# Low attention scores of the odd head pairs in the other two quadrants of TensorE, and their part of y behind U

## The chip, the cores and the metric

The kernel runs on one core of one Trainium2 chip. The metric is device time in microseconds (us), the median of several executions; lower is better. PE is TensorE, DVE VectorE, ACT ScalarE, POOL GpSimd, SP SyncE.

## What is computed

A gated linear attention of 4 sequences with 8 heads of 48 channels over 768 steps, and two MLPs on its output, all in fp32:

```python
for t in range(S):                       # state: 48x48 per head
    state = alpha[t][:, None] * state + k[t] (outer) v[t]
    y[t] = q[t] @ state
x = y                                    # 3072 tokens x 384
x = (h - tanh(h)) @ w_out                # h = x @ w_in, 384 -> 2048 -> 384
out = leaky(x @ w2_in) @ w2_out          # slope alpha2 per channel for h < 0
```

## The kernel before

**Tiles.** Attention is done in 24 tiles: tile g holds 128 time steps of one of the four sequences, with its 8 heads as four pairs (p = 0 to 3); of a pair, head u = 0 has its channels in partitions 0 to 63 and head u = 1 in 64 to 127. The steps of a tile are done at once: running products of alpha (`attn_a1`, `attn_a2`) scale q on POOL (L235) and k on DVE (L247), so that plain matmuls do the rest:
- scores (`attn_sc`): k against q, then on DVE a causal mask (`attn_m`), which gives P;
- y (`attn_y`): the state of the tiles before times q, plus v times P;
- the update U of the state (`attn_u`): k times v, then on DVE the new state (`attn_s`);
- x: y is copied on ACT (`attn_xh`, L445) and what the copy rounded off is taken on DVE (`attn_xl`, L452).

Tiles 8 to 23 are the halved ones (`halved`). There the 128x128 scores of a head are three 64x64 blocks; the fourth would be masked away. The late 64 steps against both halves of the earlier ones are the high scores (L284). The early 64 steps against themselves are the low scores (L288).

**Places on PE.** PE's array is used in parts: a matmul with 64 rows of k and 64 columns of result takes one of four quadrants, told by the partitions that it reads (rows) and those of PSUM that it writes (columns). High scores go round all four. Low scores of head u read partitions 64u and write partitions 64u, so that they use two, the other two stay unused. For y, 64x32 tiles hold the first 32 channels of a head against the state (L383) and against the low scores (L391, with `vlow`, a copy of v's early steps laid out for both halves), and 128x32 tiles hold the rest (L396 to L405) and U (L437).

**PSUM.** Banks 0, 1, 2 are used whole by the halved tiles (`shared`); high scores lie in banks 1 and 2, low scores in bank 0, y in 1 and 2, U in 0. Banks 3 to 7 belong to the MLPs.

**Order.** Every engine works through its instructions in the order of the program, which is written out by hand: a loop over steps of the MLPs (`steps`), of each nine matmuls for h (`mm_h`, L552) and nine of the step two back into the accumulators (`mm_acc1`, L607), with the attention put between by two tables. `vec` is run ahead of the step's elementwise work and holds the scans of the next tile, `mid` behind it and holds scores, y and U. For tiles 8 to 11 `attn_a` of tile g + 1 stands in `vec` of the step whose `mid` has `piece_c` of tile g (y, U, x, state). For later tiles it stands three steps ahead of `piece_c`, and the scores of tile g + 1 stand right ahead of y of tile g.

```python
at(vec, s + 1 if j == 2 else s if g == 3 * B else s - 1, attn_a, g + 1)
at(mid, s + (1 if j == 2 else 2), piece_c, g)
```

Of the kernel before, what the change touches and what calls it, by code (L numbers as in the profile page):

```python
# [10 lines left out]
F32 = mybir.dt.float32  # L11
# [3 lines left out]
ALU = mybir.AluOpType  # L15
# [8 lines left out]
NP = H // 2  # L24
# [24 lines left out]
def c_place(h):  # L49

    return h if h < 4 else 4 + (h % 4 ^ 1)
# [84 lines left out]
def emit_all(nc, tc, const, qkav, vlow, vt, w1, w2, alpha2, cst, out):  # L136
    c = {}
    c["masks"] = const.tile([128, CH + CH // 2], F32, name="masks")
    c["mask"], c["mlow"] = c["masks"][:, 0:CH], c["masks"][:, CH:]
    c["ident"] = const.tile([128, 128], F32, name="ident")  # L140
    c["d1a"] = const.tile([128, AW], F32, name="d1a")
    c["d1s"] = const.tile([128, AW], F32, name="d1s")
    c["al2"] = const.tile([128, KF], F32, name="al2")
    c["nal"] = const.tile([128, KF], F32, name="nal")
    c["lim"] = const.tile([128, 3], F32, name="lim")
    c["out_of"] = const.tile([128, 2 * NTILE + 2 * KF + 1], F32, name="out_of")
    c["sums"] = const.tile([128, 2 * KF], F32, name="sums")
    c["guard"] = const.tile([128, 4], F32, name="guard")
    c["flag"] = const.tile([1, 1], U32, name="flag")

    with tc.tile_pool(name="x2d", bufs=1, space=DRAM) as dp:
        x2d = [dp.tile([128, KC, N2], F32, name=f"x2d{j}") for j in range(NB)]
        c["bad2d"] = dp.tile([128, 1], F32, name="bad2d")
        engines = mybir.EngineType
        tc.mark_branch_hint_location("general", "LikelyTaken",
                                     [engines.PE, engines.SP, engines.Activation, engines.DVE])
        emit_fast(nc, tc, qkav, vlow, w1, w2, alpha2, cst, out, x2d, c)

    with tc.If(c["bad"] > 0, label="general"):
        emit_general(nc, tc, qkav, vt, w1, w2, c["al2"], cst, out)  # L160


def emit_fast(nc, tc, qkav, vlow, w1, w2, alpha2, cst, out, x2d, c):
# [14 lines left out]
    def bank(i, shape, name):  # L178
        return ps.tile(shape, F32, tag=f"bank{i}", name=name)
# [82 lines left out]
    def shared(b):  # L262

        if b not in shared_t:
            shared_t[b] = bank(b, [128, 512], "all")
        return shared_t[b]

    def attn_banks(g):

        if g < B:  # L270
            return ((7, 2, 3, 3)[g], (5, 6) if g % 2 == 0 else (0, 1), (7, 2)[g // 2], 256 * (g % 2))
        if g < 2 * B:
            return 5, (6, 7), 5, 0
        return 0, (1, 2), 0, 0

    def attn_sc(g):
        _, q, k, _ = qk_t[g]
        if halved(g):
            scs = st[g, "sc"] = [shared(b)[:, 0:NP * HC].rearrange("s (p t) -> s p t", p=NP) for b in (1, 2, 0)]
            for p in range(NP):  # L280
                for u in range(2):
                    r = 64 * u
                    for t in (0, HC):
                        nc.tensor.matmul(scs[u][t:t + HC, p], k[r:r + 64, p, t:t + HC], q[r:r + 64, p, HC:CH],  # L284
                                         start=True, stop=True)
            for p in range(NP):
                for r in (0, 64):
                    nc.tensor.matmul(scs[2][r:r + 64, p], k[r:r + 64, p, 0:HC], q[r:r + 64, p, 0:HC],  # L288
                                     start=True, stop=True)
            return  # L290
        scs = [bank(b, [128, NP, CH], f"sc{u}") for u, b in enumerate(attn_banks(g)[1])]
        for p in range(NP):
            for u in range(2):
                r = 64 * u
                nc.tensor.matmul(scs[u][:, p], k[r:r + 64, p], q[r:r + 64, p], start=True, stop=True)
        st[g, "sc"] = scs
# [32 lines left out]
    def last_tile(g):  # L329
        return g >= NTILE - B  # L330

    HC = CH // 2
    vl_t = {}

    def halved(g):
# [4 lines left out]
    def load_vlow(g):  # L340
# [2 lines left out]
        vl = vl_t[g] = bp.tile([128, NP, 64], F32, tag="vlow", name="vlow")  # L343
        nc.sync.dma_start(vl.rearrange("s p e -> s (p e)"), vlow[g - 2 * B])

    def attn_m(g):
        scs = st.pop((g, "sc"))
        if halved(g):
            tiles = [bp.tile([128, 2, NP, HC], F32, tag="P0", name="P0"), bp.tile([128, 1, NP, HC], F32, tag="P1", name="P1")]
            st[g, "P", 0], st[g, "P", 1], st[g, "P", 2] = P = tiles[0][:, 0], tiles[1][:, 0], tiles[0][:, 1]  # L350
            for i, m in enumerate((mask[:, HC:CH], mask[:, HC:CH], mlow)):
                nc.vector.tensor_tensor(P[i], scs[i], m[:, None, :].to_broadcast([128, NP, HC]), op=ALU.mult)
            return
        for u in range(2):
            P = bp.tile([128, NP, CH], F32, tag=f"P{u}", name=f"P{u}")
            nc.vector.tensor_tensor(P, scs[u], mask[:, None, :].to_broadcast([128, 4, CH]), op=ALU.mult)  # L356
            st[g, "P", u] = P

    def attn_y(g):
        _, q, _, v = qk_t[g]  # L360
# [4 lines left out]
        if first:  # L365
            y = bank(b0, [128, KC, CH], "y")
            parts = st[g, "y"] = ((y, slice(0, KC)),)
            y = [y[:, ct] for ct in range(KC)]
        else:
            if halved(g):  # L370
                even, odd = (shared(b)[:, 256:256 + n * CH].rearrange("r (n t) -> r n t", n=n)
                             for b, n in ((1, 2), (2, 1)))
            else:
                even, odd = bank(b0, [128, 2, CH], "y"), bank(b1, [128, 1, CH], "y")
            st[g, "y"] = (even, slice(0, KC, 2)), (odd, slice(1, 2))
            y = [even[:, 0], odd[:, 0], even[:, 1]]

        if not first:
            for i in range(4):
                for ct in range(2):  # L380
                    h = c_place(4 * ct + i)
                    p, r = h // 2, 64 * (h % 2)
                    nc.tensor.matmul(y[ct][32 * i:32 * i + 32], Sp[r:r + 64, p, 0:32], q[r:r + 64, p],  # L383
                                     start=True, stop=False)
        if halved(g):
            vl, Pl = vl_t.pop(g), st.pop((g, "P", 2))
            for i in range(4):
                for ct in range(2):
                    h = c_place(4 * ct + i)
                    p, r = h // 2, 64 * (h % 2)  # L390
                    nc.tensor.matmul(y[ct][32 * i:32 * i + 32, 0:HC], vl[r:r + 64, p, 0:32], Pl[r:r + 64, p],  # L391
                                     start=False, stop=False)
            for ct in range(2):
                for i in range(4):
                    h = c_place(4 * ct + i)
                    nc.tensor.matmul(y[ct][32 * i:32 * i + 32, HC:CH], v[:, h // 2, h % 2, 0:32], P[h % 2][:, h // 2],  # L396
                                     start=False, stop=(ct == 1))
            for u in range(2):
                for p in range(NP):
                    nc.tensor.matmul(y[2][32 * p:32 * p + 32, HC:CH], v[:, p, u, 32:64], P[u][:, p],  # L400
                                     start=False, stop=False)
            for p in range(NP):
                nc.tensor.matmul(y[2][32 * p:32 * p + 32, 0:HC], vl[:, p, 32:64], Pl[:, p], start=False, stop=False)
            for p in range(NP):
                nc.tensor.matmul(y[2][32 * p:32 * p + 32], Sp[:, p, 32:64], q[:, p], start=False, stop=True)  # L405
            return
        for ct in range(2):
            for i in range(4):
# [13 lines left out]
    def attn_u(g):  # L422
        if last_tile(g):
            return
        v = qk_t[g][3]
        knat = st.pop((g, "knat"))
        _, _, b, o = attn_banks(g)
        if halved(g):
            u_bank[b] = shared(b)
            o = 256  # L430
        elif o == 0:
            u_bank[b] = bank(b, [128, 512], "U")
# [530 lines left out]

    def close(g):
        attn_y(g)
        attn_u(g)
        attn_xh(g)


# [318 lines left out]
def pack(inputs):  # L1288
# [20 lines left out]
    vlow = vp.reshape(NTILE, CH, NP, 2, 64)[2 * B:, 0:CH // 2].transpose(0, 3, 1, 2, 4).reshape(-1, CH, NP * 64)  # L1309
# [30 lines left out]
```

## Time and profile before

| | |
|---|---|
| median of 3 runs | 887.82 us (887.74 to 888.15) |
| the profiled execution | 888.66 us |
| its span in the profile | 886.8 us |
| PE busy | 876.6 us (99%) |
| DVE, ACT, POOL busy | 639.7 (72%), 485.3 (55%), 90.4 us (10%) |
| chain that ended last: PE, DVE, ACT | 89%, 6%, 2% |

A row of the timeline gives the start and the length of a run of like instructions on one engine; lengths of matmuls are modelled, so that matmuls are read by their starts. An fp32 matmul is two records. PEld is the load of weights into PE.

### The profile page before, as it was taken

What the parts mean: (1) busy time and instruction counts of PE and PEld (TensorE: products, weight loads), DVE (VectorE), ACT (ScalarE), POOL (GpSimd) and SP (SyncE); (2) the same over time, 40 slices, a digit from 0 to 9 for tenths busy, and PEclk for the clock granted to TensorE, in tenths of its full rate; (3) what the DMA queues carried; (4) which work ended last, traced back from release to release, by engine and by line L of the source; (5) the groups of instructions that cost most, each with busy time, mean ns of one, the idle gap of its engine ahead of it and who ended that gap; (6) DMA issues with size and microseconds to landing.
All of it is one profiled execution on the core that took longest, in us unless ns stands there. A gap on an engine that the chain in (4) does not pass through costs nothing.

```text
span 886.8 us, 16995 instructions
## 1 busy us (share of the span) xinstructions
PE 876.6 (99%) x6960; PEld 726.5 (82%) x6966; DVE 639.7 (72%) x1120; ACT 485.3 (55%) x908; POOL 90.4 (10%) x89
## 2 busy tenths in 40 slices
PE   8999999999999999999999999999999999999997
PEld 5678887888888888888888888888888888888886
DVE  8998996777556665553467798796867776867774
ACT  3565645555656566533677664454554554554542
POOL 2100000110000100000125234010010010010000
PEclk9999999999999999999999999999999999999999
DMA  9675003345455544300563211001001000100001
GB/s 335 257 294 223 1 1 87 104 123 174 138 169 189 179 142 140 121 7 10 202 211 119 103 77 36 36 1 37 36 2 36 36 8 30 36 1 1 36 1 37
DMA packets 34946, 83.70 MB, mean 94 GB/s; under 512 B 15409, under 2 KB 17970, under 8 KB 32306
## 3 DMA queue, kind: packets, MB, share of 16 engines
q1 hardware_dynamic: 21906, 79.28, 24.9%
q10 hardware_dynamic: 12960, 3.31, 2.0%
q8 instruction: 55, 0.90, 0.4%
q14 instruction: 25, 0.20, 0.1%
HBM read 70.00 MB, written 9.44 MB: 90 GB/s over the span
## 4 chain that ended last, share of the span: by engine, by line
PE 89%; DVE 6%; ACT 2%; DMA 1%; issue 1%; ACTq 0%
PE h L552 41%; PE acc L607 20%; PE o L749 18%; PE o L628 4%; PE all L284 1%; DVE iA L245 1%; DMA qv<-qkav 1%; DVE cv L102 1%; PE all L288 1%; DVE P L356 1%; DVE cv L101 1%; DVE A L233 1%; PE all L383 1%; PE all L396 1%; PE all L437 1%
## 5 line engine op out<-in xcount | busy, mean ns | idle before, releaser
L552 PE MATMUL h<-x,w 128*128 128x512 f32 x1728 | 489.9, 391 | 0.0
L552 PEld LDWEIGHTS h<-x,w 128*128 128x128 f32 x1728 | 324.1, 188 | 68.8
L607 PE MATMUL acc<-g,w 128*128 128x512 f32 x864 | 214.9, 393 | 0.3 <-ACT x2e L616 0.3
L607 PEld LDWEIGHTS acc<-g,w 128*128 128x128 f32 x864 | 160.2, 188 | 35.3 <-issue 0.8
L749 PE MATMUL o<-g,w 128*128 128x256 f32 (+1 forms) x625 | 172.6, 335 | 0.0
L590 DVE TENSOR_TENSOR g<-gb,g 128x512 fp32r<-128x512 f32 x120 | 85.7, 714 | 53.1 <-ACT g L585 52.6
L749 PEld LDWEIGHTS o<-g,w 128*128 128x128 f32 x625 | 111.9, 188 | 14.5
L585 ACT CAST g<-gb 128x512 fp32r<-128x512 f32 x120 | 74.5, 621 | 89.7 <-DVE gb L567 56.4
L567 DVE TENSOR_TENSOR gb<-h,ga 128x512 f32<-128x512 f32 x96 | 66.1, 689 | 73.9 <-ACT ga L566 73.3
L749 PE MATMUL o<-g,ws 128*128 128x256 f32 x408 | 113.8, 279 | 0.0
L573 DVE SCALAR_TENSOR_TENSOR gb<-h,ga 128x512 f32<-128x512 f32 x80 | 55.2, 690 | 70.1 <-ACT ga L572 70.1
L572 ACT ACTIVATE ga<-h,nal 128x512 f32<-128x512 f32 x80 | 55.1, 688 | 77.0 <-PE h L552 76.6
L566 ACT ACTIVATE ga<-h 128x512 f32<-128x512 f32 x96 | 56.8, 591 | 67.0 <-PE h L552 66.9
L704 ACT CAST g<-gb 128x512 fp32r<-128x512 f32 x72 | 44.8, 622 | 61.5 <-DVE gb L573 60.2
L749 PEld LDWEIGHTS o<-g,ws 128*128 128x128 f32 x408 | 76.9, 188 | 0.0
L235 POOL TENSOR_TENSOR qkav_t<-qkav_t,A 128x512 f32<-128x512 f32 x20 | 24.7, 1234 | 312.4 <-DVE ac L234 293.5
L702 DVE TENSOR_TENSOR g<-gb,g 128x512 fp32r<-128x512 f32 x72 | 49.3, 685 | 3.0 <-ACT g L704 2.8
L905 POOL TENSOR_TENSOR x<-x2f,x 128x512 fp32r<-128x512 f32 x18 | 24.4, 1358 | 235.7 <-ACT x L904 141.5
L93 POOL TENSOR_TENSOR w<-cv,w 128x384 fp32r<-128x384 f32 x32 | 35.5, 1130 | 111.2 <-DVE g L590 66.8
L106 ACT CAST w<-cv 128x768 fp32r<-128x768 f32 x32 | 26.7, 835 | 27.0 <-DVE cv L102 27.0
L245 DVE TENSOR_TENSOR_SCAN iA<-qkav_t,d1s 128x516 f32<-128x516 f32 x20 | 36.2, 1809 | 0.7
L101 DVE SCALAR_TENSOR_TENSOR cv<-raw,cv 128x768 uint32<-128x768 uint32 x32 | 35.2, 1100 | 0.1
(145 smaller groups left out, 895.5 us busy)
## 6 DMA issues: line engine op xcount, KB each, us to landing
raw<-w SPq DMA_DIRECT2D x48, 768.0 KB, 5.4
qkav_t<-qkav SPq DMA_DIRECT2D x20, 1028.0 KB, 5.6
x2d<-x2e SPq DMA_DIRECT2D x18, 256.0 KB, 2.3
out<-oe SPq DMA_DIRECT2D x17, 256.0 KB, 2.1
x2f<-x2d SPq DMA_DIRECT2D x15, 256.0 KB, 3.6
qv<-qkav SPq DMA_DIRECT2D x8, 256.0 KB, 7.7
vlow<-vlow SPq DMA_DIRECT2D x16, 128.0 KB, 2.8
ak<-qkav SPq DMA_DIRECT2D x3, 516.0 KB, 7.3
```

The lines of the kernel that those rows point to most:

```text
L245: lambda: nc.vector.tensor_tensor_scan(iA[:, AW - 1:0:-1], a[:, AW - 1:0:-1], d1s[:, AW - 1:0:-1], 1.0, op0=ALU.mult, op1=ALU.add),
L552: ops = [lambda k=k, a=a, b=b, ct=ct: nc.tensor.matmul(h, w[:, a, ct * 128:(ct + 1) * 128], x[:, b, ct, :], start=(k == 0), stop=(k == 8)) ...
L566: nc.scalar.activation(ga, h, ACTF.Tanh)
L567: nc.vector.tensor_tensor(gb, h, ga, op=ALU.subtract)
L572: nc.scalar.activation(ga, h, ACTF.Relu, scale=c["nal"][:, f:f + 1])
L573: nc.vector.scalar_tensor_tensor(gb, h, 0.0, ga, op0=ALU.max, op1=ALU.subtract)
L585: nc.scalar.copy(g[:, 0], gb)
L590: chains.append([lambda: nc.vector.tensor_tensor(g[:, 1], gb, g[:, 0].bitcast(F32), op=ALU.subtract)])
L607: nc.tensor.matmul(acc[j][c], w[:, a, DM + c * 128:DM + (c + 1) * 128], g[:, b, :], start=(first and i == 0), stop=(last and i == 2))
L702: v.tensor_tensor(g[:, 1], gb, g[:, 0].bitcast(F32), op=ALU.subtract)
L704: nc.scalar.copy(g[:, 0], gb)
L749: ops.append(lambda a=a, b=b, i=i, n=n: nc.tensor.matmul(out[:, n], w(a), g(b)[:, n], start=(start and i == 0), stop=(stop and i == 2)))
```

## The change

The low scores of odd pairs write the partitions of the other half, `low_row(p, u) = 64 * (u ^ p % 2)`: with the even pairs they go round all four quadrants. Those of even pairs lie in bank 2, of odd pairs in bank u. All three banks get the same areas: scores in columns 0 to 255 (U in bank 2), low scores in 256 to 383, y in 384 to 511, each third of y in a bank of its own. `vlow` is packed with the two heads of odd pairs exchanged.

On DVE the low products are three instructions (even pairs; odd pairs of either half). In y the low part of the first 32 channels comes last, behind U. As it now may run in another half of the rows than the state's part of the same result, a memset of one element on POOL (`token`) waits for the last state matmul, and the first low matmul waits for the memset. x is copied, and its rest taken, in three pieces instead of two.

```diff
 def attn_sc(g):
-            scs = st[g, "sc"] = [shared(b)[:, 0:NP * HC].rearrange("s (p t) -> s p t", p=NP) for b in (1, 2, 0)]
+            high = [shared(u)[:, SC].rearrange("s (p t) -> s p t", p=NP) for u in range(2)]
+            low = [shared(b)[:, LO].rearrange("s (p t) -> s p t", p=NP // 2) for b in range(3)]
...
             for p in range(NP):
-                for r in (0, 64):
-                    nc.tensor.matmul(scs[2][r:r + 64, p], k[r:r + 64, p, 0:HC], q[r:r + 64, p, 0:HC],
+                for u in range(2):
+                    r, t = 64 * u, low_row(p, u)
+                    b = u if p % 2 else 2
+                    nc.tensor.matmul(low[b][t:t + HC, p // 2], k[r:r + 64, p, 0:HC], q[r:r + 64, p, 0:HC],
                                      start=True, stop=True)
...
+    def low_row(p, u):
+        return 64 * (u ^ p % 2)
...
 def attn_m(g):
-            for i, m in enumerate((mask[:, HC:CH], mask[:, HC:CH], mlow)):
-                nc.vector.tensor_tensor(P[i], scs[i], m[:, None, :].to_broadcast([128, NP, HC]), op=ALU.mult)
+            for u in range(2):
+                nc.vector.tensor_tensor(Ph[:, u], high[u], m, op=ALU.mult)
+            for rows, b, p in ((slice(0, 128), 2, 0), (slice(64, 128), 0, 1), (slice(0, 64), 1, 1)):
+                nc.vector.tensor_tensor(Pl[rows, p:NP:2], low[b][rows],
+                                        mlow[rows, None, :].to_broadcast([rows.stop - rows.start, NP // 2, HC]),
+                                        op=ALU.mult)
...
 def attn_y(g):
-            for i in range(4):
-                for ct in range(2):
-                    h = c_place(4 * ct + i)
-                    p, r = h // 2, 64 * (h % 2)
-                    nc.tensor.matmul(y[ct][32 * i:32 * i + 32, 0:HC], vl[r:r + 64, p, 0:32], Pl[r:r + 64, p],
-                                     start=False, stop=False)
+            passed = nc.gpsimd.memset(c["token"], 0.0)
+            tc.add_manual_dep(passed.ins, state.ins.name, behind, reason="row tiles")
...
+            attn_u(g)
+            for i in range(4):
+                for ct in range(2):
+                    h = c_place(4 * ct + i)
+                    p, r = h // 2, low_row(h // 2, h % 2)
+                    low = nc.tensor.matmul(y[ct][32 * i:32 * i + 32, 0:HC], vl[r:r + 64, p, 0:32], Pl[r:r + 64, p],
+                                           start=False, stop=True)
+                    if i == ct == 0:
+                        tc.add_manual_dep(low.ins, passed.ins.name, behind, reason="row tiles")
...
 def close(g):
     attn_y(g)
-    attn_u(g)
+    if not halved(g):
+        attn_u(g)
     attn_xh(g)
...
 def pack(inputs):
+    vlow[:, :, :, 1:NP:2] = vlow[:, ::-1, :, 1:NP:2].copy()
```

POOL's instructions from the multiplication of q of tile 8 on (L235 before, L236 now; `qkav_t_776`, `_882`, `_971` are tiles 8, 9, 10, in the change `_777`, `_883`, `_972`). Before:

```order
L235 TENSOR_TENSOR qkav_t_776<-qkav_t_776,A_1490 128x512
L235 TENSOR_TENSOR qkav_t_882<-qkav_t_882,A_1620 128x512
L235 TENSOR_TENSOR qkav_t_971<-qkav_t_971,A_1825 128x512
L235 TENSOR_TENSOR qkav_t_1699<-qkav_t_1699,A_2017 128x512
L235 TENSOR_TENSOR qkav_t_1903<-qkav_t_1903,A_2183 128x512
```

In the change:

```order
L236 TENSOR_TENSOR qkav_t_777<-qkav_t_777,A_1491 128x512
L236 TENSOR_TENSOR qkav_t_883<-qkav_t_883,A_1623 128x512
L404 MEMSET token_70 1x1
L236 TENSOR_TENSOR qkav_t_972<-qkav_t_972,A_1833 128x512
L404 MEMSET token_70 1x1
L236 TENSOR_TENSOR qkav_t_1705<-qkav_t_1705,A_2030 128x512
L404 MEMSET token_70 1x1
```

Behind the multiplication of tile 9 stands the memset of tile 8, behind that of tile 10 the memset of tile 9, and so on.

PE's instructions of y and U of tile 8. Before (L383 state, L391 low part, L396 to L403 v times P, L405 state's last 16 channels, L437 U):

```order
L383 MATMUL all<-qkav_t,S_282 32x128 x8
L391 MATMUL all<-P_1588,vlow 32x64 x8
L396 MATMUL all<-P_1588,qkav_t 32x64
L396 MATMUL all<-P_1589,qkav_t 32x64
...
L400 MATMUL all<-P_1588,qkav_t 32x64 x4
L400 MATMUL all<-P_1589,qkav_t 32x64 x4
L403 MATMUL all<-P_1588,vlow 32x64 x4
L405 MATMUL all<-qkav_t,S_282 32x128 x4
L437 MATMUL all<-qkav_t,knat 32x64 x16
L607 MATMUL acc_1043<-g,w 128x512 x3
```

In the change (L400 state, L409 and L415 v times high P, L412 state's last channels, L418 the low part's last channels, L458 U, L424 the low part, L628 the MLP):

```order
L400 MATMUL all<-qkav_t,S_283 32x128 x8
L409 MATMUL all<-P_1589,qkav_t 32x64 x8
L412 MATMUL all<-qkav_t,S_283 32x128 x4
L415 MATMUL all<-P_1589,qkav_t 32x64 x8
L418 MATMUL all<-P_1590,vlow 32x64 x4
L458 MATMUL all<-qkav_t,knat 32x64 x16
L424 MATMUL all<-P_1590,vlow 32x64 x8
L628 MATMUL acc_1044<-g,w 128x512 x3
```

The low part (eight matmuls with `vlow`) has gone from behind the state's part to behind U.

DVE's instructions from P of tile 8 to the scan of A of tile 9 (L233, L234 in the change; named SCALAR_TENSOR_TENSOR there, TENSOR_TENSOR_SCAN in the profile). Before:

```order
L352 TENSOR_TENSOR P_1588<-all,masks 128x256
L352 TENSOR_TENSOR P_1589<-all,masks 128x256
L352 TENSOR_TENSOR P_1588<-all,masks 128x256
L590 TENSOR_TENSOR g<-gb,g 128x512
L233 SCALAR_TENSOR_TENSOR A<-qkav_t,d1a 128x517
```

In the change:

```order
L363 TENSOR_TENSOR P_1589<-all,masks 128x256 x2
L365 TENSOR_TENSOR P_1590<-all,masks 128x2x64
L365 TENSOR_TENSOR P_1590<-all,masks 64x2x64 x2
L611 TENSOR_TENSOR g<-gb,g 128x512
L234 SCALAR_TENSOR_TENSOR A<-qkav_t,d1a 128x517
```

Three products have become five; what follows stands as it did.

## Rows read from the trace of the kernel before

**Rows 1.** page: busy time of each engine; granted clock of PE in 40 slices.
```profile
PE 876.6 (99%) x6960; PEld 726.5 (82%) x6966; DVE 639.7 (72%) x1120; ACT 485.3 (55%) x908; POOL 90.4 (10%) x89
...
PEclk9999999999999999999999999999999999999999
```

**Rows 2.** PE's timeline at tiles 8 to 12: start us, us, line, out<-in, records, [idle before].
```profile
142.22 0.45 PE L383 MATMUL all<-qkav_t,S 64*32 64x128 f32 x16
...
153.91 2.34 PE L607 MATMUL acc<-g,w 128*128 128x512 f32 x9 [0.29 <-ACT x2e L616]
...
158.22 0.45 PE L383 MATMUL all<-qkav_t,S 64*32 64x128 f32 x16
...
173.87 0.45 PE L383 MATMUL all<-qkav_t,S 64*32 64x128 f32 x16
...
185.43 0.45 PE L383 MATMUL all<-qkav_t,S 64*32 64x128 f32 x16
...
206.24 0.45 PE L383 MATMUL all<-qkav_t,S 64*32 64x128 f32 x16
```

**Rows 3.** PE's timeline: scores of tile 16, y and U of tile 15.
```profile
263.61 0.69 PE L284 MATMUL all<-qkav_t 64*64 64x64 f32 x32
264.12 0.65 PE L288 MATMUL all<-qkav_t 64*64 64x64 f32 x16
264.70 0.45 PE L383 MATMUL all<-qkav_t,S 64*32 64x128 f32 x16
264.94 0.32 PE L391 MATMUL all<-P,vlow 64*32 64x64 f32 x16
265.19 0.43 PE L396 MATMUL all<-P,qkav_t 128*32 128x64 f32 x16
...
265.99 0.63 PE L437 MATMUL all<-qkav_t,knat 128*32 128x64 f32 x32
266.55 0.73 PE L607 MATMUL acc<-g,w 128*128 128x512 f32 x2
```

**Rows 4.** the same in narrow windows: the last record of L288, L383 and L437.
```profile
264.55 0.22 PE L288 MATMUL all<-qkav_t 64*64 64x64 f32 x1
...
264.88 0.27 PE L383 MATMUL all<-qkav_t,S 64*32 64x128 f32 x1
...
266.40 0.22 PE L437 MATMUL all<-qkav_t,knat 128*32 128x64 f32 x1
```

**Rows 5.** POOL's timeline: multiplication of q for tiles 9 to 13.
```profile
145.54 1.19 POOL L235 TENSOR_TENSOR qkav_t<-qkav_t,A 128x512 f32<-128x512 f32 x1 [11.66 <-DVE ac L234]
161.09 1.19 POOL L235 TENSOR_TENSOR qkav_t<-qkav_t,A 128x512 f32<-128x512 f32 x1 [14.36 <-DVE ac L234]
174.45 1.19 POOL L235 TENSOR_TENSOR qkav_t<-qkav_t,A 128x512 f32<-128x512 f32 x1 [12.17 <-DVE ac L234]
186.21 1.19 POOL L235 TENSOR_TENSOR qkav_t<-qkav_t,A 128x512 f32<-128x512 f32 x1 [10.57 <-DVE ac L234]
197.27 1.19 POOL L235 TENSOR_TENSOR qkav_t<-qkav_t,A 128x512 f32<-128x512 f32 x1 [9.87 <-DVE ac L234]
```

**Rows 6.** DVE's timeline behind P of tile 8.
```profile
143.47 0.69 DVE L590 TENSOR_TENSOR g<-gb,g 128x512 fp32r<-128x512 f32 x1 [1.34 <-ACT g L585]
144.08 1.23 DVE L233 TENSOR_TENSOR_SCAN A<-qkav_t,d1a 128x517 f32<-128x517 f32 x1
```

**Rows 7.** timelines of PE and ACT between tiles 8 and 9.
```profile
146.25 2.20 PE L552 MATMUL h<-x,w 128*128 128x512 f32 x9
...
149.70 0.59 ACT L566 ACTIVATE ga<-h 128x512 f32<-128x512 f32 x1
```

**Rows 8.** POOL's timeline: one of the first memsets of one column.
```profile
1.22 0.10 POOL L940 MEMSET lim<- 128x1 f32 x1
```

**Rows 9.** PE's weight loads at the start, and its longest idle time.
```profile
5.97 0.15 PEld L949 LDWEIGHTS <-idle_w 128*128 128x128 bf16 x1 [0.28 <-issue]
...
11.70 0.53 PE L410 MATMUL y<-P,qv 128*32 128x128 f32 x12 [1.70 <-DMA qv<-qkav]
```

More of the change, by code (lines that the diff above doesn't have):

```diff
@@ L148, in emit_all @@
     c["guard"] = const.tile([128, 4], F32, name="guard")
+    c["token"] = const.tile([1, 1], F32, name="token")
     c["flag"] = const.tile([1, 1], U32, name="flag")
@@ L266, in shared @@
         return shared_t[b]
+    HC = CH // 2
+    SC, LO, Y = slice(0, NP * HC), slice(256, 256 + NP * HC // 2), slice(384, 512)
     def attn_banks(g):
@@ L271, in attn_banks @@
             return ((7, 2, 3, 3)[g], (5, 6) if g % 2 == 0 else (0, 1), (7, 2)[g // 2], 256 * (g % 2))
-        if g < 2 * B:
-            return 5, (6, 7), 5, 0
-        return 0, (1, 2), 0, 0
+        return 5, (6, 7), 5, 0
     def attn_sc(g):
@@ L283, in attn_sc @@
                     for t in (0, HC):
-                        nc.tensor.matmul(scs[u][t:t + HC, p], k[r:r + 64, p, t:t + HC], q[r:r + 64, p, HC:CH],
+                        nc.tensor.matmul(high[u][t:t + HC, p], k[r:r + 64, p, t:t + HC], q[r:r + 64, p, HC:CH],
                                          start=True, stop=True)
             for p in range(NP):
-                for r in (0, 64):
-                    nc.tensor.matmul(scs[2][r:r + 64, p], k[r:r + 64, p, 0:HC], q[r:r + 64, p, 0:HC],
+                for u in range(2):
+                    r, t = 64 * u, low_row(p, u)
+                    b = u if p % 2 else 2
+                    nc.tensor.matmul(low[b][t:t + HC, p // 2], k[r:r + 64, p, 0:HC], q[r:r + 64, p, 0:HC],
                                      start=True, stop=True)
+            st[g, "sc"] = high, low
             return
@@ L330, in last_tile @@
         return g >= NTILE - B
-    HC = CH // 2
     vl_t = {}
@@ L348, in attn_m @@
         if halved(g):
-            tiles = [bp.tile([128, 2, NP, HC], F32, tag="P0", name="P0"), bp.tile([128, 1, NP, HC], F32, tag="P1", name="P1")]
-            st[g, "P", 0], st[g, "P", 1], st[g, "P", 2] = P = tiles[0][:, 0], tiles[1][:, 0], tiles[0][:, 1]
-            for i, m in enumerate((mask[:, HC:CH], mask[:, HC:CH], mlow)):
-                nc.vector.tensor_tensor(P[i], scs[i], m[:, None, :].to_broadcast([128, NP, HC]), op=ALU.mult)
+            high, low = scs
+            Ph = bp.tile([128, 2, NP, HC], F32, tag="P0", name="P0")
+            Pl = bp.tile([128, NP, HC], F32, tag="P1", name="P1")
+            st[g, "P", 0], st[g, "P", 1], st[g, "P", 2] = Ph[:, 0], Ph[:, 1], Pl
+            m = mask[:, None, HC:CH].to_broadcast([128, NP, HC])
+            for u in range(2):
[4 more added lines that the diff above has]
+                                        op=ALU.mult)
             return
@@ L357, in attn_m @@
             st[g, "P", u] = P
+    behind = mybir.DependencyInfo(mybir.DependencyClass.Sync, mybir.DependencyReason.DATA)
     def attn_y(g):
@@ L370, in attn_y @@
             if halved(g):
-                even, odd = (shared(b)[:, 256:256 + n * CH].rearrange("r (n t) -> r n t", n=n)
-                             for b, n in ((1, 2), (2, 1)))
+                y = [shared(ct)[:, Y] for ct in range(KC)]
+                st[g, "y"] = tuple((y[ct], ct) for ct in (2, 0, 1))
             else:
                 even, odd = bank(b0, [128, 2, CH], "y"), bank(b1, [128, 1, CH], "y")
-            st[g, "y"] = (even, slice(0, KC, 2)), (odd, slice(1, 2))
-            y = [even[:, 0], odd[:, 0], even[:, 1]]
+                st[g, "y"] = (even, slice(0, KC, 2)), (odd, slice(1, 2))
+                y = [even[:, 0], odd[:, 0], even[:, 1]]
         if not first:
@@ L382, in attn_y @@
                     p, r = h // 2, 64 * (h % 2)
-                    nc.tensor.matmul(y[ct][32 * i:32 * i + 32], Sp[r:r + 64, p, 0:32], q[r:r + 64, p],
-                                     start=True, stop=False)
+                    state = nc.tensor.matmul(y[ct][32 * i:32 * i + 32], Sp[r:r + 64, p, 0:32], q[r:r + 64, p],
+                                             start=True, stop=False)
         if halved(g):
             vl, Pl = vl_t.pop(g), st.pop((g, "P", 2))
-            for i in range(4):
-                for ct in range(2):
-                    h = c_place(4 * ct + i)
-                    p, r = h // 2, 64 * (h % 2)
-                    nc.tensor.matmul(y[ct][32 * i:32 * i + 32, 0:HC], vl[r:r + 64, p, 0:32], Pl[r:r + 64, p],
-                                     start=False, stop=False)
+            passed = nc.gpsimd.memset(c["token"], 0.0)
+            tc.add_manual_dep(passed.ins, state.ins.name, behind, reason="row tiles")
             for ct in range(2):
@@ L396, in attn_y @@
                     nc.tensor.matmul(y[ct][32 * i:32 * i + 32, HC:CH], v[:, h // 2, h % 2, 0:32], P[h % 2][:, h // 2],
-                                     start=False, stop=(ct == 1))
+                                     start=False, stop=False)
+            for p in range(NP):
+                nc.tensor.matmul(y[2][32 * p:32 * p + 32], Sp[:, p, 32:64], q[:, p], start=True, stop=False)
             for u in range(2):
@@ L402, in attn_y @@
             for p in range(NP):
-                nc.tensor.matmul(y[2][32 * p:32 * p + 32, 0:HC], vl[:, p, 32:64], Pl[:, p], start=False, stop=False)
-            for p in range(NP):
-                nc.tensor.matmul(y[2][32 * p:32 * p + 32], Sp[:, p, 32:64], q[:, p], start=False, stop=True)
+                nc.tensor.matmul(y[2][32 * p:32 * p + 32, 0:HC], vl[:, p, 32:64], Pl[:, p], start=False, stop=True)
+            attn_u(g)
[7 more added lines that the diff above has]
+                        tc.add_manual_dep(low.ins, passed.ins.name, behind, reason="row tiles")
             return
@@ L428, in attn_u @@
         if halved(g):
[L429 to L432, printed above, removed]
+            b, o = 2, 0
+        if o == 0:
+            u_bank[b] = shared(b) if halved(g) else bank(b, [128, 512], "U")
         U = u_bank[b][:, o:o + NP * 64].rearrange("d (p e) -> d p e", p=NP)
@@ L1308, in pack @@
         qkav[:, :, AP + i * 512:AP + (i + 1) * 512] = x.reshape(NTILE, 128, 512)
-    vlow = vp.reshape(NTILE, CH, NP, 2, 64)[2 * B:, 0:CH // 2].transpose(0, 3, 1, 2, 4).reshape(-1, CH, NP * 64)
+    vlow = vp.reshape(NTILE, CH, NP, 2, 64)[2 * B:, 0:CH // 2].transpose(0, 3, 1, 2, 4).copy()
+    vlow[:, :, :, 1:NP:2] = vlow[:, ::-1, :, 1:NP:2].copy()
+    vlow = vlow.reshape(-1, CH, NP * 64)
     vt = np.ascontiguousarray(v.transpose(0, 1, 3, 2).reshape(B * NP, 2 * D, S))
```

## The prediction, made before the change was run

> **What bounds the kernel now.** I read the page first, then the timeline of TensorE (PE) over one attention tile, then the same stretch on POOL, VectorE (DVE) and ScalarE (ACT). On the page the reader is to see that PE is busy 99% of the span while POOL is at 10%, and that every slice of PE's granted clock is at 9 tenths or more [rows 1]. So what PE is spared is gained, and what PE waits is lost. Of the 16 changed tiles only tile 9 shows PE idle, for 0.29 us [rows 2].
>
> One tile in the middle shows what the change touches [rows 3]. An fp32 matmul stands there as two records. The high scores (L284) are 32 records in 264.12 - 263.61 = 0.51 us. The low scores (L288) are half as many, 16, and take longer: 264.70 - 264.12 = 0.58 us. The last of the 16 starts at 264.55 [rows 4], so they start over 0.43 us, and 0.15 us more goes by until PE works in the next shape of tile: that is what a change of shape costs behind the last record of the old one, and it is so behind U as well (266.40 to 266.55 [rows 3, 4]). High scores go round four places of the array (two halves of its rows by two of its columns), low scores round two. In rounds, the first are 8 rounds of four records, the second 8 rounds of two, at about 0.06 us a round both.
>
> **Scores: a gain.** After the change the eight low matmuls go round four places, so 16 records are 4 rounds instead of 8. From first to last start 7 rounds lie in 0.43 us less some 0.02, so a round is 0.058 us; four fewer save 0.23 us a tile, 16 times: **-3.7 us**. Bounds: nothing, if the new places don't overlap with the old ones, and 0.26 us, if the 16 took half of the high scores' 0.51 and the switch were part of neither. I take 0.23, since the high scores show four places at work.
> The Trainium skill, page TensorE: Matmul & The Clock Gate, section Measured speedup vs the span model, lets each further tile of a packed round add about 4 ns. By it a round of four is 8 ns longer than one of two, an estimate of 0.03 us a tile, and the whole sum would come out 0.5 us higher. The rows show a round of four at 0.51/8 = 0.064 with its start-up in it, which leaves room for either.
>
> **y: one change of shape more.** Before, the state's part and the low part (64x32 tiles both) stand together, and everything with 128x32 tiles follows. Now the low part stands behind U. In the middle, the switch then follows the state's last record, which starts at 264.88 and lasts 0.27 us where one of 64 columns lasts 0.22 [rows 4]; so the switch takes 0.05 us longer than 0.15 and ends at 265.08 instead of 265.19: 0.11 saved. At the end come a switch of 0.15 into 64x32 and two rounds at 0.06, 0.27 in all; the switch back to 128x128 is paid behind U now. Net 0.16 us a tile, 16 times: **+2.6 us**. Bounds: 0, if U's last round hides the switch, and 0.27, if the middle saves nothing.
>
> **The token: a wait of PE on POOL.** The low part no longer follows the state's part in the same places of the array, so a memset on POOL waits for the state's last matmul and the first low matmul waits for the memset. Counted from the first state matmul, PE would reach the low part after 265.08 - 264.70 = 0.38 us for the state, 266.40 - 265.19 = 1.21 us to U's last record and 0.15 us for the switch: **1.74 us**. A memset takes 0.10 us [rows 8]; with an estimated 0.05 until PE sees it, 0.15 (bounds 0.1 and 0.3). For the last twelve tiles that is hidden: at tile 12 the state starts at 206.24, and the multiplication of q of tile 13 that stands ahead on POOL began at 197.27 [rows 2, 5].
> For tiles 8 to 11, POOL's order puts the q multiplication of the next tile ahead of the memset too, but there it starts after the state's part: at 145.54 for a y at 142.22, 161.09 for 158.22, 174.45 for 173.87, 186.21 for 185.43, 1.19 us each [rows 2, 5]. At tile 8 nothing lets it come earlier: it follows the scan of A on DVE at 144.08, which follows the g at 143.47, for which DVE had waited 1.34 us on ACT [rows 6].
> - Tile 8: PE is at the low part at 142.22 - 0.23 + 1.74 = 143.73; the token is there at 145.54 + 1.19 + 0.15 = 146.88: **3.15 us** of idle. PE is then 3.15 - 0.23 + 0.16 = 3.08 us late.
> - Tile 9: in the rows of before the token would be (161.09 + 1.19 + 0.15) - (158.22 + 1.74) = 2.47 late. PE comes 3.08 - 0.23 - 0.29 = 2.56 later; the 0.29 is its old wait for ACT's x2e copies, which falls away. POOL comes later by less: ACT's tanh at 149.70 needs the h that PE ends at 146.25 + 2.20 = 148.45 [rows 7]; 3.08 later that is 151.53, so ACT, DVE's scan behind it and POOL shift by 1.85. 2.47 + 1.85 - 2.56 leaves **1.76 us**.
> - Tiles 10 and 11: the same difference gives 0.18 and 0.38, and faster scores bring PE 0.23 earlier; but POOL's chain again shifts by less than PE. Between 0 and 0.61 each; I take **0.36**, twice.
>
> Together +5.6 us, less tile 9's 0.3. Behind the waiting memset on POOL stands only the q multiplication of the tile after next, some 14 us later [rows 5]; behind the waiting matmul on PE stands the whole MLP.
>
> **What costs nothing.** DVE gets five products for P instead of three, two of them extra and narrower; if each took even the 0.69 us of a 512-wide one, 1.4 us stand against the 1.34 that DVE idles just behind them [rows 6]. ACT copies x, and DVE takes its rest, in three pieces instead of two; both engines are off PE's path (72% and 55% busy [rows 1]). Without that cover one piece more on each would be up to 0.7 us a tile. vlow is read 1 us later than before, so its next load starts as much later.
>
> **Sum:** -3.7 + 2.6 + 5.6 - 0.3 = **+4.2 us**. The profiled execution took 888.66 us around a span of 886.8, 0.84 above the median of the runs, 887.82. So 892.9 in its own terms and **892.0 us** against the median.
>
> **Rivals.**
> 1. *The token is in time* (the other side). With q of the next tile through POOL before PE is at the low part, no idle arises: -3.7 + 2.6 = -1.1 us, 886.7; if the extra switch were free too, 884.1. For it: tiles 12 to 23 stand so. Against: at tile 8 the multiplication would have to end 3 us before its row. It decides where the four stalls together are under 1.4 us.
> 2. *The low scores stay at two a time*: the 3.7 us don't come, 887.8 + 7.9 = 895.7. For it: in the even pairs both halves of rows still write one bank. Against: so do the low scores of before, whose rounds of two are no longer than the high scores' of four.
> 3. *The clock falls in tile 8's idle time.* At 5.97 us of the span, loads for 512-column matmuls stand 0.15 + 0.28 = 0.43 us apart, the lower level of 1.2 GHz [rows 9]; in steady work nine such matmuls take 2.20 us [rows 7], 0.24 each. Some 5 us at the lower level, as at the start, lose half, +2.5: 894.5. Against: an idle of 1.70 us near 10 us [rows 9] shows no slice with less than 9 tenths. But 3.15 is longer than any idle of this trace. The Trainium skill, page TensorE: Matmul & The Clock Gate, section Part 1: The HAM clock gate, says that an array left idle goes back to 1.2 GHz, which speaks against this change; no row here shows that in mid-kernel.
> 4. *The extra switch is free*: 2.6 us less, 889.4. For it: U's records are short. Against: U's exit at 0.15.
>
> **How the numbers follow.** Forecast 0.60, rival 1 0.13 (of it 0.06 with a gain that can be told), rival 2 0.08, rival 3 0.11, rival 4 0.08. About 0.2%, 1.8 us, is what a measurement of this kernel can tell from no change. Slower: 0.60 + 0.08 + 0.11 and the 0.02 of rival 4 in which the stalls are larger, 0.81. Within: 0.07 of rival 1 and 0.06 of rival 4, 0.13. Faster: 0.06. The range goes from rival 4, a little below for the bounds of the later stalls, 889.0, to rival 2, 895.8, and leaves out rival 1.
>
> **What would show it.** Right: PE idle ahead of the first low matmul of y, released by POOL, for some 3 us at tile 8, 1 to 2.5 at tile 9, under 0.7 at 10 and 11 and not at all from tile 12; low scores in about 0.35 us with their switch; y with U 0.16 us longer. Wrong: no such idle, low scores still at 0.58 us, or a clock below full in the slice behind tile 8.

## The result, and the profile after

The changed kernel takes 894.31 us (median of 10 executions, 891.95 to 900.08) against 888.37 for the kernel before in the same comparison (10 executions): a ratio of 1.007, with a 95% interval of 1.0049 to 1.0091. It is slower, as forecast; 894.31 lies inside the range of 889.0 to 895.8, 2.3 us above the predicted 892.0.

Two things are mixed in it. Each execution comes with the mean clock that was granted to TensorE. The lowest executions, 891.95 and 892.19, had 0.999 and 1.0. The others go up with the clock that they lost: 893.23, 893.73 and 893.99 at 0.998, 894.63, 894.79 and 896.28 at 0.996, 898.07 at 0.993, 900.08 at 0.991. So the changed kernel takes 892 at full clock, and 1 to 8 us more in 8 of 10 executions.

The profiled execution is the 891.95 (span 890.1, against 888.66 and 886.8 before). Busy times and granted clock on its page, to be laid beside [rows 1]:

```profile
PE 876.2 (98%) x6966; PEld 722.5 (81%) x6966; DVE 647.4 (73%) x1168; ACT 488.5 (55%) x924; POOL 90.7 (10%) x105
...
PEclk9999999999999999999999999999999999999999
```

PE works as long as before, in a span 3.3 us longer: it waits. PE's timeline at tiles 8, 9 and 11 shows where (start, length, idle time before in brackets):

```profile
142.43 0.76 PE L400 MATMUL all<-qkav_t,S 64*32 64x128 f32 x16 [0.33 <-DVE P L365]
143.12 0.43 PE L409 MATMUL all<-P,qkav_t 128*32 128x64 f32 x16
...
146.84 0.35 PE L424 MATMUL all<-P,vlow 64*32 64x64 f32 x16 [2.29 <-POOL token L404]
147.12 2.35 PE L628 MATMUL acc<-g,w 128*128 128x512 f32 x9
149.31 1.07 PE L573 MATMUL h<-x,w 128*128 128x512 f32 x4
...
163.37 0.35 PE L424 MATMUL all<-P,vlow 64*32 64x64 f32 x16 [0.88 <-POOL token L404]
...
191.57 0.35 PE L424 MATMUL all<-P,vlow 64*32 64x64 f32 x16 [0.84 <-POOL token L404]
```

In the kernel before, the MLP behind tiles 8 and 11 stood at

```profile
144.07 2.34 PE L607 MATMUL acc<-g,w 128*128 128x512 f32 x9
...
187.28 2.34 PE L607 MATMUL acc<-g,w 128*128 128x512 f32 x9
```

and in the changed kernel it stands at 147.12 and at

```profile
191.84 2.34 PE L628 MATMUL acc<-g,w 128*128 128x512 f32 x9
```

The first low matmul (L424) waits for the memset. POOL's timeline shows why, beside [rows 5]:

```profile
145.59 1.17 POOL L236 TENSOR_TENSOR qkav_t<-qkav_t,A 128x512 f32<-128x512 f32 x1 [11.66 <-DVE ac L235]
146.70 0.09 POOL L404 MEMSET token<- 1x1 f32 x1
162.12 1.18 POOL L236 TENSOR_TENSOR qkav_t<-qkav_t,A 128x512 f32<-128x512 f32 x1 [15.33 <-ACT ga L587]
163.23 0.09 POOL L404 MEMSET token<- 1x1 f32 x1
...
190.31 1.18 POOL L236 TENSOR_TENSOR qkav_t<-qkav_t,A 128x512 f32<-128x512 f32 x1 [11.21 <-ACT ga L587]
191.43 0.09 POOL L404 MEMSET token<- 1x1 f32 x1
...
210.98 0.09 POOL L404 MEMSET token<- 1x1 f32 x1 [8.05 <-PE all L400]
```

At tiles 8, 9 and 11 the memset starts right behind the multiplication of q of the next tile; at tile 12 (210.98) nothing stands ahead of it and it follows PE's state part. A tile of the middle, to be laid beside [rows 3]:

```profile
267.72 0.69 PE L287 MATMUL all<-qkav_t 64*64 64x64 f32 x32
268.24 0.41 PE L293 MATMUL all<-qkav_t 64*64 64x64 f32 x16
268.58 0.45 PE L400 MATMUL all<-qkav_t,S 64*32 64x128 f32 x16
268.96 0.43 PE L409 MATMUL all<-P,qkav_t 128*32 128x64 f32 x16
...
269.76 0.63 PE L458 MATMUL all<-qkav_t,knat 128*32 128x64 f32 x32
270.32 0.34 PE L424 MATMUL all<-P,vlow 64*32 64x64 f32 x16
270.59 2.33 PE L628 MATMUL acc<-g,w 128*128 128x512 f32 x9
```

The low scores (L293) take 268.58 - 268.24 = 0.34 us where they took 0.58. From the state's part to the MLP it is 270.59 - 268.58 = 2.01 us where it was 266.55 - 264.70 = 1.85.

The two traces can be laid over each other matmul by matmul, since the MLPs' matmuls are the same ones in the same order. The lag of the changed kernel is how much later such a matmul starts in it. Ahead of tile 8 it is 0.03 us; behind that it moves only at the attention tiles:

| place | step of the lag, us |
|---|---|
| scores of tiles 8, 10, 11 and 12, each | -0.21 to -0.23 |
| y and U of tile 8 | +3.23 |
| wait for x2e ahead of tile 9's y, gone (its scores in the figure) | -0.60 |
| y and U of tile 9 | +1.11 |
| y and U of tile 10 | +0.37 |
| y and U of tile 11 | +1.08 |
| tiles 12 to 22 (scores and y together), each | -0.07 |
| y of tile 23 (no scores behind it) | +0.16 |
| lag at the end, with the 0.03 from ahead of tile 8 | +3.70 |

### The profile page after: what moved, and what is told of

It is laid out like the page before. It is cut to its first block, busy times and chain, and to the rows that moved or that the text cites. A ratio compares the mean times of both kernels' runs of the same rounds, so it can differ in the third digit from the quotient of the medians.

```text
span 890.1 us, 17082 instructions
## 1 busy us (share of the span) xinstructions
PE 876.2 (98%) x6966; PEld 722.5 (81%) x6966; DVE 647.4 (73%) x1168; ACT 488.5 (55%) x924; POOL 90.7 (10%) x105
## 4 chain that ended last, share of the span: by engine, by line
PE 78%; DVE 0%; issue 0%
PE h L573 37%; PE o L770 18%; PE acc L628 16%; PE o L649 4%; PE all L287 1%; PE all L400 1%; PE all L409 0%; PE all L424 0%; PE all L458 0%; PE all L293 0%; PE all L415 0%; PE all L412 0%; PE all L418 0%; DVE oe L809 0%
## 5 line engine op out<-in xcount | busy, mean ns | idle before, releaser
L628 PE MATMUL acc<-g,w 128*128 128x512 f32 x864 | 214.9, 393 | 0.0
L628 PEld LDWEIGHTS acc<-g,w 128*128 128x128 f32 x864 | 160.2, 188 | 34.5
L236 POOL TENSOR_TENSOR qkav_t<-qkav_t,A 128x512 f32<-128x512 f32 x20 | 23.7, 1186 | 188.1 <-DVE ac L235 89.3
```

Source lines behind the costliest of these rows:

```text
L628: nc.tensor.matmul(acc[j][c], w[:, a, DM + c * 128:DM + (c + 1) * 128], g[:, b, :], start=(first and i == 0), stop=(last and i == 2))
```

## The experiments

**Theory 1**: PE waits for a token that stands behind the multiplication of q on POOL, and that idle time also costs the clock in part of the executions. **Theory 2**: the multiplication is not what counts, and the four quadrants and the additional change of shape cost the clock or more time than they save. The first four kernels ran on one chip, beside 16 executions of the kernel before with a median of 888.65 us; the second four on another, beside 17 with a median of 888.42.

### Multiplication of q behind the memset

In tiles 9 to 12 the multiplication is issued only after y and U of the tile before.

```diff
 def attn_a1(g):
+        if 2 * B < g <= 3 * B:
+            st[g, "q later"] = ops.pop()
         return ops
 def piece_c(g):
         close(g)
+        if (g + 1, "q later") in st:
+            st.pop((g + 1, "q later"))()
```

> The change, with one thing undone on POOL: for tiles 9 to 12 the multiplication of q is put behind the memset of the tile before. Theory 1 (PE waits for a token that stands behind that multiplication, and the clock is lost in that idle time): the waits of 2.3, 0.9 and 0.8 us of PE go, the work of the 16 tiles is 16 x (0.16 - 0.23) = -1.1 us against before, the granted clock is 1.0 in every run: about 887.2 us, ratio 0.998 to 1.000, and single runs as close together as before's. Theory 2 (the scores in four quadrants or the additional change of shape cost the clock, not the wait): runs still spread over several us with clocks down to 0.99, median 890 to 892.

Measured: 888.01 us (11 executions), ratio 0.9992 (0.9983 to 1.0001), where the changed kernel has 1.007. No low matmul of any tile waits for the token any more. POOL's timeline of this kernel at tile 8:

```profile
144.93 0.09 POOL L406 MEMSET token<- 1x1 f32 x1 [9.38 <-PE all L402]
147.11 1.20 POOL L236 TENSOR_TENSOR qkav_t<-qkav_t,A 128x512 f32<-128x512 f32 x1 [2.09 <-ACT x L468]
```

The stalls came from the place in POOL's order; with them gone, scores in four quadrants and y's new order together take no time that the runs can tell from none. No wait of PE behind the multiplication that now starts later shows in this profile. The clock is not at 1.0 in every execution, as Theory 1 had it: 3 of 11 had 0.997 or 0.998, against 3 of 16 of the kernel before on that chip. The profiled execution is one of the three; its clock falls to 0.50 near 14 us, behind an idle of 2.11 us at the start of the kernel, and not behind tile 8. One wait is left, PE's timeline at tile 8:

```profile
144.06 0.76 PE L402 MATMUL all<-qkav_t,S 64*32 64x128 f32 x16 [0.33 <-DVE P L367]
144.75 0.43 PE L411 MATMUL all<-P,qkav_t 128*32 128x64 f32 x16
```

The state's part waits 0.33 us before it starts and takes 144.75 - 144.06 = 0.69 us instead of the 0.38 of tile 15, so that 0.33 + 0.31 = 0.64 us go to waiting for DVE's five products. The changed kernel has the same (0.33 and 143.12 - 142.43 = 0.69), hidden there by the wait for the token behind it. With it the tiles' steps in the lag add up to -0.8 us and not to the -1.1 that was expected.

### The order of y alone

The kernel before, with the low part behind U; low scores, banks and vlow as before, no token.

```diff
-            for i in range(4):
-                for ct in range(2):
...
+            attn_u(g)
+            for i in range(4):
+                for ct in range(2):
+                    h = c_place(4 * ct + i)
+                    p, r = h // 2, 64 * (h % 2)
+                    nc.tensor.matmul(y[ct][32 * i:32 * i + 32, 0:HC], vl[r:r + 64, p, 0:32], Pl[r:r + 64, p],
+                                     start=False, stop=True)
```

> The kernel before, with the low part of y put behind U and nothing else (same quadrants, no token, no wait). Theory 1: +0.16 us a tile by the additional change of shape, 16 tiles, +2.6 us: about 890.9, ratio 1.003, clock 1.0, runs close together. Theory 2 (the additional change of shape costs the clock): more than that, with runs spread and clocks under 1.0.

Measured: 891.39 us (6 executions), ratio 1.0029 (1.0017 to 1.0042). In the profile each of the 16 tiles adds 0.16 us to the lag. PE's timeline, from the state's part of tile 15 to the MLP:

```profile
266.14 0.45 PE L383 MATMUL all<-qkav_t,S 64*32 64x128 f32 x16
266.52 0.43 PE L390 MATMUL all<-P,qkav_t 128*32 128x64 f32 x16
...
267.88 0.34 PE L405 MATMUL all<-P,vlow 64*32 64x64 f32 x16
268.15 1.20 PE L608 MATMUL acc<-g,w 128*128 128x512 f32 x4
```

268.15 - 266.14 = 2.01 us, as in the changed kernel. The extra switch is real, and rival 4 (it is free) falls.

### PE's idle time filled, all of it or part

Matmuls of no use, 128x256, into columns that nobody reads, ahead of the low part: 16 in tile 8, 5 each in tiles 9 and 11; then those of tile 8 alone, and those of tiles 9 and 11 alone. Nothing else is changed.

```diff
+            for _ in range({2 * B: 16, 2 * B + 1: 5, 2 * B + 3: 5}.get(g, 0)):
+                nc.tensor.matmul(shared(0)[:, 0:256], w_t[1, 0][:, 0, 0:128], x_t[0][:, 0, 0, 0:256],
+                                 start=False, stop=False, skip_group_check=True)
```

> The change, with matmuls put into PE's waits of tiles 8, 9 and 11 (16, 5 and 5 of 128x256, into columns of a bank whose contents are no longer used; they add nothing to the result). The token still comes when it came. Theory 1: the clock stays at 1.0, so that every run is at what the fastest runs of the change are, about 892 us, within 1.5 us of each other; ratio 1.004. Theory 2: clocks and spread as in the change, median about 894.

> The changed kernel with 16 matmuls of no use (into columns of a bank that nobody reads) where PE waits at tile 8 alone; the waits of tiles 9 (0.88) and 11 (0.84) stay idle. Theory 1: no fall of the clock behind tile 8 in any execution, the executions lie close together, as with all three waits filled, at 892 to 894.5, granted clock 0.999 or more. Theory 2 (the clock is lost at any of the waits, or elsewhere): executions scatter as those of the changed kernel do, some with a mean granted clock under 0.998.

> The changed kernel with 5 matmuls of no use in each of the waits of tiles 9 and 11; the 2.3 us of tile 8 stay idle. Theory 1: executions scatter as those of the changed kernel do, some under 0.998 of granted clock and 1 to 4 us above the lowest. Theory 2 (the waits of tiles 9 and 11 cost the clock): they lie close together at 0.999.

Measured: all three filled 894.57 us (5 executions, 893.76 to 894.78), tile 8 alone 894.43 (4, 893.64 to 894.72), tiles 9 and 11 alone 896.16 (4, 894.60 to 896.46). The clock separates as Theory 1 has it: with tile 8 filled all 9 executions had 0.999, with tile 8 idle all 4 had 0.997 or 0.998. The granted clock right behind tile 8 (windows view: the window, its length, busy times of PE, PEld, DVE, ACT, POOL, then the clock, DMA share and GB/s), in the kernel with tiles 9 and 11 filled, where PE idles 2.28 us at tile 8:

```profile
130.00:144.00 14.00, 13.66 (x139) 10.59 (x141) 9.55 (x18) 7.66 (x15) 1.20 (x1) 1.00 0.10 19
147.50:151.00 3.50, 3.50 (x25) 2.72 (x10) 3.43 (x9) 1.06 (x3) 0.00 (x0) 0.55 0.57 167
151.50:156.00 4.50, 4.50 (x21) 3.70 (x21) 0.79 (x2) 1.53 (x2) 0.00 (x0) 1.00 0.19 80
```

and with tile 8 filled:

```profile
147.50:151.00 3.50, 3.50 (x17) 2.89 (x16) 3.39 (x9) 0.63 (x2) 0.00 (x0) 1.00 0.76 242
```

The times themselves missed: the filled kernels stood at 893.6 or more, not at 892, so the fillers tell of the clock and not of the time. In the lag, the kernel with tile 8 filled loses 2.4 us at two places where it has no filler. PE's timeline there:

```profile
192.56 0.35 PE L427 MATMUL all<-P,vlow 64*32 64x64 f32 x16 [2.04 <-POOL token L404]
...
292.00 0.31 PE L427 MATMUL all<-P,vlow 64*32 64x64 f32 x7 [0.96 <-issue]
```

and ACT's at tile 11, of the changed kernel and of this one:

```profile
186.61 1.17 ACT L321 COPY knat<-kturn 128x1024 uint16<-128x1024 uint16 x1 [0.61 <-DMA kturn<-kflat]
...
187.60 1.17 ACT L321 COPY knat<-kturn 128x1024 uint16<-128x1024 uint16 x1 [1.81 <-DMA kturn<-kflat]
```

The first is tile 11's token again, 1.20 us longer than in the changed kernel: ACT's copy of knat (k transposed, for U), and behind it everything up to POOL, waited 1.81 us for the DMA that transposes k into kturn, where the changed kernel waited 0.61. The granted clock stayed at 1.00 behind these 2.04 us. The second has no releaser in the trace; all three filled kernels show one such wait of 0.6 to 1.1 us, between 290 and 312 us, and neither the changed kernel nor the kernel before does. Its cause stays open. With all three filled, PE's last run of matmuls starts 1.05 us later than in the changed kernel's profile (879.86 and 878.81) but the span ends 2.7 us later; why the end takes longer is open too.

### PE idle for longer

Four memsets of 128x256 on POOL ahead of tile 8's token.

```diff
+            if g == 2 * B:
+                for _ in range(4):
+                    nc.gpsimd.memset(c["pad"], 0.0)
             passed = nc.gpsimd.memset(c["token"], 0.0)
```

> The change, with four more memsets of 256 columns on POOL ahead of the token of tile 8, so that PE's wait there is 1 to 2 us longer. Theory 1: the added idle time, and the clock falls in more runs and for longer: median 897 us or more, and a profile with a stretch at the lower of the two levels behind tile 8. Theory 2: only the added idle time, median about 895.5, clocks as in the change.

Measured: 895.12 us (4 executions, 894.84 to 895.77), every one at 0.997 or 0.998. PE is idle at tile 8 for 3.64 us instead of 2.29, and the clock falls behind it:

```profile
148.65 0.35 PE L428 MATMUL all<-P,vlow 64*32 64x64 f32 x16 [3.64 <-POOL token L408]
```

In the windows behind it:

```profile
149.50:152.50 3.00, 3.00 (x9) 2.33 (x8) 2.08 (x7) 0.64 (x2) 0.00 (x0) 0.50 0.76 233
153.50:157.00 3.50, 3.50 (x17) 2.87 (x16) 0.69 (x1) 1.53 (x2) 0.00 (x0) 1.00 0.05 21
```

Over tile 8 its lag on the changed kernel's profile grows by 2.9 us; 1.35 of it is idle time (3.64 - 2.29) and the rest the clock. The time came out near Theory 2's 895.5 and not at the 897 or more of Theory 1, though the clock fell as Theory 1 says: one fall costs less than Theory 1 had assumed.

### The changed kernel again

> The changed kernel as it is, beside the two partly filled kernels on one chip. Theory 1 (PE stands idle behind POOL's token at tiles 8, 9 and 11, and the clock falls in the 2.3 us idle time of tile 8 in some executions, not in all): full-clock executions at 892, others 1 to 4 us above them with a granted clock under 0.998 on average; median 893 to 894.5; where the profile holds a fall it stands within 5 us behind 147. Theory 2 (the clock falls at other places, for the row tiles or by chance): executions with a fall are as frequent in the kernel before, and the fall of a profile stands elsewhere.

Measured: 894.01 us (6 executions, 892.04 to 896.07), ratio 1.0061 (1.0049 to 1.0074). One execution had 1.0 and took 892.04; the others had 0.998 (893.76 to 894.19) or 0.996 (895.18 and 896.07). This time the profile is of a 0.996. PE's timeline behind the 2.29 us:

```profile
147.93 0.35 PE L424 MATMUL all<-P,vlow 64*32 64x64 f32 x16 [2.29 <-POOL token L404]
148.21 3.91 PE L628 MATMUL acc<-g,w 128*128 128x512 f32 x9
151.96 1.31 PE L573 MATMUL h<-x,w 128*128 128x512 f32 x5
```

and the windows:

```profile
148.50:151.50 3.00, 3.00 (x8) 2.32 (x8) 2.93 (x8) 0.92 (x3) 0.00 (x0) 0.50 0.63 197
152.50:156.00 3.50, 3.50 (x17) 2.88 (x16) 0.69 (x1) 1.53 (x2) 0.00 (x0) 1.00 0.14 59
```

The stretch behind tile 8 in the first profile, with the same idle of 2.29 us ahead of it, has

```profile
147.50:151.00 3.50, 3.50 (x17) 2.87 (x16) 3.43 (x9) 0.83 (x3) 0.00 (x0) 1.00 0.69 232
```

Nine MLP matmuls take 151.96 - 148.21 = 3.75 us where that profile has 149.31 - 147.12 = 2.19: 1.56 us for one fall to the level of 1.2 GHz. The second fall of this execution is at the start, behind an idle of 2.04 us (timeline, then a window):

```profile
11.55 0.88 PE L432 MATMUL y<-P,qv 128*32 128x128 f32 x16 [2.04 <-DMA qv<-qkav]
```

```profile
12.00:14.50 2.50, 2.50 (x41) 2.00 (x33) 2.44 (x4) 0.48 (x1) 0.06 (x1) 0.50 1.04 427
```

That wait, for a DMA, is in every kernel here and differs from execution to execution: it was 1.70 us in [rows 9], with no fall behind it. So lost clock meets kernels without the idle of tile 8 too: 7 of 33 executions of the kernel before on the two later chips had 0.998 or less, 1 of 6 with the order of y alone, 6 of 22 of the two kernels with q's multiplication behind the memset and none of the 9 with tile 8 filled, 14 of 70 in all. Of the changed kernel it is 13 of 16.

### A candidate: the even pairs' low product last

The kernel with q's multiplication behind the memset, and DVE's low products in another order, so that banks 0 and 1, to which the state's part is written, come free first.

```diff
-            for rows, b, p in ((slice(0, 128), 2, 0), (slice(64, 128), 0, 1), (slice(0, 64), 1, 1)):
+            for rows, b, p in ((slice(64, 128), 0, 1), (slice(0, 64), 1, 1), (slice(0, 128), 2, 0)):
```

> The kernel with q's multiplication behind the token, and of the three low products of DVE the one of the even pairs (bank 2) last instead of first. At tile 8 PE's state matmuls waited 0.33 us and again some 0.3 for low products that read the banks that y is written to. If DVE's order of products is the cause: y of tile 8 is some 0.3 us shorter, other tiles unchanged, 887.4 at full clock, 0.9988 of before. If not (the sum of the five products is what counts, or another engine): no change of tile 8, 887.7 at full clock.

Measured: 887.84 us (11 executions, 887.21 to 889.01), ratio 0.9992 (0.9984 to 1.0001). The time does not decide between the two expectations (887.4 and 887.7); the trace does. At tile 8 the lag on the kernel before now grows by 0.64 us at y instead of 0.87, so the order of the products is part of the cause; the four products that have to end before the state's part is done are still two more than before. Tile 11 gave 0.2 back (its y added 0.36 us instead of 0.16); why is open. The two candidates lie 0.6 us under the kernel before by their medians, each with an interval that ends at 1.0001: about what the tiles' steps in the lag add up to (0.8 and 0.9), but no gain that the runs can tell from none.

## Why the prediction was right, and where it was not

**The stalls (+5.6 us): the mechanism was right, the sizes of the small ones were off.** PE's wait at tiles 8 to 11 and not later is what the rows show, and moving the multiplication of q behind the token takes the whole loss away. Tile 8: the first low matmul was forecast at 146.88 and stands at 146.84; PE 3.08 us late forecast, 3.05 - 0.03 = 3.02 measured. The idle row itself has 2.29 and not "some 3", since PE came to the low part later than forecast, after 0.64 us of waiting for DVE. Tile 9: forecast 1.76 us, measured 1.11 - 0.16 = 0.95. The step that failed is that POOL shifts by as much as ACT, 1.85: its multiplication came 162.12 - 161.09 = 1.03 later. (By the text's own rows the 1.85 is 151.53 - 149.70 = 1.83, which changes nothing.) ACT did shift by 1.85 (its copy of k ahead of the transposing DMA from 150.19 to 152.04), but the issue of that DMA took 1.25 us instead of 1.98, and the copies of x2e behind it came only 154.40 - 153.28 = 1.12 later. Tile 10: 0.36 forecast, 0.37 - 0.16 = 0.21 measured. Tile 11: 0.36 forecast, 1.08 - 0.16 = 0.92 measured. The step that failed there is "POOL's chain again shifts by less than PE": it shifted by more (190.31 - 186.21 = 4.10 against 3.5), since ACT stood 0.61 us at a transposing DMA for which it had not waited before. So the idle rows of tiles 9 and 11, 0.88 and 0.84, fall outside what the text gave for a right forecast (1 to 2.5, and under 0.7). With tile 8 at 3.23 - 0.16 = 3.07 the four make 3.07 + 0.95 + 0.21 + 0.92 = 5.15. The old wait for x2e went, worth 0.60 - 0.23 = 0.37 (0.3 forecast).

**Scores (-3.7 us): right.** 0.58 - 0.34 = 0.24 in the rows, 0.23 in the lag of each tile. A round of four is not visibly longer than one of two. The 0.20 that would have been left by the Trainium skill's 4 ns for each further tile (page TensorE: Matmul & The Clock Gate, section Measured speedup vs the span model) is not what these tiles show, if the change of shape behind the scores costs what it did; the trace then disagrees with it here, by 0.03 us a tile. Rival 2 (still two at a time) is out.

**y (+2.6 us): right.** 2.01 - 1.85 = 0.16 us a tile in the changed kernel and alone, 16 times 2.6. For tiles 12 to 22 the two terms make the -0.07 of the table.

**What was to cost nothing: one row was missed.** The term set DVE's five products against the time that DVE idles behind them. But PE does not wait for DVE's next work, it waits for the products: y's first two thirds now lie in banks from which four of the five products read, and at tile 8, where P is made right ahead of y, that took 0.64 us. In the changed kernel it lies inside the 3.07 above (PE would else have reached the token that much earlier and waited for it there); with the token in time it shows. The copies of x in three pieces made no wait.

**The sum, at full clock.** Forecast +4.2. The terms measured: -3.7 + 2.6 + 5.15 - 0.37 = +3.7, the lag at the end of the table; the span grew by 3.3, since 0.3 less stands behind PE's last matmul, in no term of the sum. The executions at full clock, 891.95, 892.04 and 892.19, stand at the forecast 892.0, in part by luck: the forecast starts from 887.82, where the kernel before took 888.37 beside the changed one, and its sum of 4.2 lies 0.5 above the measured 3.7. The median of 894.31 lies in the range by another road: the range reaches up to 895.8 for rival 2, which did not happen, and what lifted the median by 2 us was the clock.

**The clock (rival 3): mis-weighed, and its price too high.** It had 0.11 of the chance; 13 of 16 executions lost clock, against 14 of 70 in the kernels without that idle, on top of the forecast mechanism, and so the median became 894. A clock below full behind tile 8 was also one of the text's signs of a wrong forecast; a profiled execution of the changed kernel shows it. The step that failed is the argument against it, that an idle of 1.70 us shows no slice with less than 9 tenths: one row of one execution, and a slice of 22 us averages a short fall away (the page of the profile with two falls has 9 in every slice as well). Behind 2.04 us at the start and 2.29 us at tile 8 there were falls, behind 2.29 us in another profile there was none, and with 3.64 us all four executions had lost clock. One fall cost 1.56 us, where the text had 2.5: 892 and one fall are 893.6, and the rival's 894.5 lies near the median because 7 of the 16 executions, at 0.996 or less, lost more than one fall costs. The Trainium skill, page TensorE: Matmul & The Clock Gate, section Part 1: The HAM clock gate, says that an idle array goes back to 1.2 GHz; the windows behind tile 8, at 0.50, agree. The same section lets the gate's monitor run on its own time, not tied to the start of a kernel, which would let the same idle end either way; no run here shows that by itself.

**Rival 1 (token in time)** was not so, but priced at -1.1 us it is nearly the kernel with q's multiplication moved: 0.6 us under the kernel before.

## What to carry to other kernels

A semaphore passed through an engine that "has time" comes when that engine's queue lets it: look at what stands ahead of it in program order and when that can start, not at the engine's share of busy time. TensorE's idle time of 2.3 us cost 1.56 us more through the clock in two of three profiles here and nothing in the third, so a forecast for a new stall carries both prices, and several executions with their granted clocks say which one came. Where writes move to banks that another engine still reads, look at which of its reads have to end first: here another order of them took 0.23 us off a wait of 0.64.

## What the runs showed of the hardware that was not expected

The clock was lost after idle times of PE of 2.04 us (start) and 2.29 us (tile 8), and not in every execution with the same idle: of three profiles with 2.28 to 2.29 us at tile 8 two show the fall, and 2.04 us at tile 11 of the kernel with tile 8 filled had none. The fall stands behind the idle time, while PE is working again: PE works from 147.93, the window from 148.50 to 151.50 has 0.50, and that from 152.50 has 1.00. The executions of the changed kernel at 0.993 and 0.991, 6 and 8 us above 892, would hold about four and five falls at 1.56 us each, an estimate; none of these was profiled, and where the others stand is open. In the three kernels with 10 to 26 matmuls added, PE has a wait of 0.6 to 1.1 us, some 100 us and more behind them, that no semaphore in the trace explains; that the added matmuls cause it is not shown.
